# Inverse rms of an attention stage stored in 16-byte pieces, with the decay of v and the rms placed later in the step

## The chip, the cores and the metric

One core of one Trainium2 chip runs the whole program. The metric is the device time of one execution in microseconds (us). Engines are named as in the profile: PE (TensorE matmul), PEld (its weight load), DVE (VectorE), ACT (ScalarE), POOL (GpSimd), SP (SyncE, which here only issues DMAs). ACT issues some DMAs too; these go to a DMA queue of their own (q10 in the profile, SP's is q1).

## The reference, cut to what matters

Three layers follow each other: a retention attention over 4 x 8 heads of 576 positions, a gated feed-forward with an rms norm in front, and a mixture of 8 experts of which each token takes one.

```python
scores = scale * np.matmul(q, k.transpose(0, 1, 3, 2))
Dmat = np.where(rel >= 0, gamma[:, None, None] ** rel[None, :, :], 0.0)
attn = np.matmul(scores * Dmat, v)            # gamma by head, rel = row - column
x = attn.transpose(0, 2, 1, 3).reshape(2304, 512)
rms = np.sqrt(np.mean(x * x, axis=-1, keepdims=True) + 1e-06)
xn = x / rms * rms_g
g = xn @ w_gate
x2 = (g * (1.0 / (1.0 + np.exp(-g))) * (xn @ w_val)) @ w_out
# then: logits -> one expert per token -> relu(x2 @ w1[e]) @ w2[e], times the gate
```

## The kernel before, in words

**The attention stage** (lines 246 to 485) handles the 4 batches one after another, each in 5 chunks of 128, 128, 128, 128 and 64 positions: 20 steps, g = 0 to 19, and a last pass g = 20 that finishes step 19. The steps of 64 positions are g = 4, 9, 14 and 19. In pass g the program gives out:

- the loads of step g + 7 (`a_load`, on SP: qk L289 or L291, vk L296), because there are 8 buffers of each,
- the decay of step g + 2 (`a_decay` L302, POOL): v times gamma to the minus position, in place,
- the scores of step g (`a_scores`: PE L313, then DVE masks them into pt, L317),
- a DMA of inverse rms values that an earlier pass has left (`a_inv` L396, issued by ACT),
- the rms of step g - 3 (`a_norm1`), which does something only at the end of a group,
- the running state of step g (`a_state`: PE L332 adds into one PSUM tile st, two ACT copies L337 and L338 take it out),
- the output of step g - 1 (`a_pv`: PE L345 and L352, DVE scales it into x, L363; ACT squares it, L365; POOL adds the squares over channels, L373 and at a group's end L375),
- one piece of the background list bg0, then the store of x of step g - 3 (`a_store` L404, SP), then a piece of weight unpacking (`a_prep`, lines 130 to 148).

**Inverse rms.** The tokens of the four steps of 128 positions of a batch form a group, the four steps of 64 a fifth one; so groups end at g = 3, 8, 13, 18 and 19. At a group's end PE sums the squares over partitions (L386), ACT and DVE make the inverse rms (L388, L389): tile ri, 128 partitions by 4 values. It is written to the DRAM tensor rinv, 512 values in a row for each group, and read back by `load_inv` (L200), spread over all 128 partitions. The first block of the next stage, x0, is normalized within the attention stage: at g = LX0 ACT issues the load of its inverse rms, and from g = NX0 on one piece of bg0 is taken in each pass: first `norm_x` (DVE, L207), then four pieces of `split_x` (ACT L220 into xh, DVE L221 into xo).

**What sets the order.** Each engine runs its instructions in the order in which the program gives them out; SP and ACT do not go past a DMA issue that waits. Every DMA of SP and ACT also counts on one of eight completion counters, DMAHW0 to DMAHW7, taken in turn, and is issued only when the DMA that had the counter before has landed. x tiles of the attention stage have 5 buffers, so that the sixth x waits for the store of the first; st is one tile, so that L332 of a step waits for the ACT copies of the step before.

**The feed-forward stage** goes over 6 blocks of 512, 512, 512, 256, 256 and 256 tokens, each in 12 slices f of the inner dimension. The first block also unpacks the weights (DVE L137 to L143, ACT, POOL). The x of block j + 1 is normalized by `norm_x` during block j, from f = 5 on, one piece for each f. The experts follow. Neither their code nor the order in the feed-forward stage is touched, apart from `load_inv` and `norm_x`.

Of the kernel before, what the change touches and what calls it, by code (L numbers as in the profile page):

```python
# [13 lines left out]
ALU = mybir.AluOpType  # L14
# [6 lines left out]
KD = DM // 128  # L21
# [4 lines left out]
BLOCKS = [512, 512, 512, 256, 256, 256]  # L26
# [13 lines left out]
SD = 3  # L40
LS = 2
FX, FN = (3, 3), (5, 5)
LX0, NX0 = 9, 11
NUA = 4
PA, PS, LD, RB = 4, 3, 8, 4
NRW = 3
# [7 lines left out]
def kernel(  # L54
# [15 lines left out]
    PE, ACT, DVE, POOL, SP = nc.tensor, nc.scalar, nc.vector, nc.gpsimd, nc.sync  # L70
# [14 lines left out]
    def ps_g(name, dt=F32):  # L85
        return psum.tile([128, 512], dt, tag="gv", name=name, bufs=3)
# [5 lines left out]
    rinv = dram.tile([NT // 512 + 1, 512], F32, name="rinv")  # L92
# [103 lines left out]
    def load_inv(j, rl, q=SP):  # L196

        gr, o = divmod(STARTS[j], 512)
        w = min(512, NT - gr * 512)
        q.dma_start(out=rl[:, :w], in_=rinv[gr:gr + 1, :w].to_broadcast([128, w]))  # L200
        return rl[:, :w].rearrange("p (c t) -> p c t", t=128)[:, o // 128:(o + BLOCKS[j]) // 128]

    def norm_x(j, xl, rl):

        def scale(c):
            x, r = xl[:, c:c + 2], rl[:, c:c + 2]
            DVE.tensor_tensor(out=x, in0=x, in1=r.unsqueeze(2).to_broadcast([128, 2, KD, 128]), op=ALU.mult)  # L207

        return [lambda c=c: scale(c) for c in range(0, BLOCKS[j] // 128, 2)]

    def x_parts():
        return [
# [33 lines left out]
    with pool("att") as att:  # L246
# [18 lines left out]
        G = len(steps)  # L265
        qk_t, vk_t, pt_t, x_t, sums, bg0, inv = {}, {}, {}, {}, {}, [], []
# [13 lines left out]
        def by_pair(ps):  # L280
            return ps.rearrange("p (a t) -> p a t", a=NP)
# [17 lines left out]
        def a_decay(g):  # L299
            b, c, o, n = steps[g]  # L300
            v3 = vk_t[g][:n, 0, :].rearrange("p (h d) -> p h d", h=H)
            POOL.tensor_tensor(  # L302
                out=v3, in0=v3, in1=vd_c[:n, c, :].unsqueeze(2).to_broadcast([n, H, D]), op=ALU.mult
            )
# [35 lines left out]
        def a_pv(g):  # L340
            b, c, o, n = steps[g]
            qk, vk, pts = qk_t.pop(g), vk_t.pop(g), pt_t.pop(g)
            pv = by_pair(ps_g("pv"))
            for p in range(NP if c else 0):
                PE.matmul(  # L345
                    pv[:, p, :n], sbd[g % 3][:, p, :], qk[:, 0, p, :n],
                    start=(p == 0), stop=False, skip_group_check=True,
                )
            for p in range(NP):
                for a in range(2):  # L350
                    h = 2 * p + a
                    PE.matmul(  # L352
                        pv[64 * a:64 * a + 64, p, :n], vk[:n, 0, h * 64:h * 64 + 64], pts[a][:n, p, :n],
                        start=(c == 0), stop=True, skip_group_check=True,
                    )
            hc, ho = home(g)
            if hc < 2 * NS0:
                x = (x0 if hc < NS0 else x1)[:, hc % NS0]
            else:
                if not ho:  # L360
                    x_t[hc] = att.tile([128, NP, 128], F32, tag="x", name="x", bufs=XB)
                x = x_t[hc][:, :, ho:ho + n]
            DVE.tensor_tensor(out=x, in0=pv[:, :, :n], in1=rc[:, c, :, :n], op=ALU.mult)  # L363
            sq = att.tile([128, NP, 128], F32, tag="sq", name="sq", bufs=4)
            ACT.activation(out=sq[:, :, :n], in_=x, func=ACTF.Square)  # L365
            gr, o = place[g]
            if not o:
                if n == 128:
                    sums[gr[0]] = att.tile([128, 2, 512], F32, tag="sqs", name="sqs", bufs=2)
                else:  # L370
                    sums[gr[0]] = att.tile([128, 2, 256], F32, name="sqh")
            s = sums[gr[0]]
            POOL.tensor_tensor(out=s[:, :, o:o + n], in0=sq[:, 0:2, :n], in1=sq[:, 2:4, :n], op=ALU.add)  # L373
            if g == gr[-1]:
                POOL.tensor_tensor(out=s[:, 0, :], in0=s[:, 0, :], in1=s[:, 1, :], op=ALU.add)  # L375

        def a_norm1(g):

            gr, o = place[g]
            if g != gr[-1]:  # L380
                return
            n, sq = o + steps[g][3], sums.pop(gr[0])[:, 0, :]
            m = n // 128
            ss = ps_g("ss")
            for i in range(m):
                PE.matmul(ss[:, i:i + 1], sq[:, i * 128:i * 128 + 128], ones, start=True, stop=True)  # L386
            ri = att.tile([128, NS0], F32, tag="ri", name="ri", bufs=2)
            ACT.activation(out=ri[:, :m], in_=ss[:, :m], func=ACTF.Sqrt, scale=1.0 / DM, bias=eps[:, 0:1])  # L388
            DVE.reciprocal(out=ri[:, :m], in_=ri[:, :m])  # L389
            i = home(gr[0])[0] // NS0  # L390
            inv.append((rinv[i:i + 1, :n].rearrange("o (c t) -> t (o c)", c=m), ri[:, :m]))

        def a_inv():

# [23 lines left out]
        for k, stages in enumerate(ua):  # L418
            g = PA + PS * k
# [26 lines left out]
        for g in range(G + 1):  # L446
            if g + QB - 1 < G:
                a_load(g + QB - 1)
            if g + 2 < G:
                a_decay(g + 2)  # L450
            if g + 1 < len(CHUNKS):
                o, n = CHUNKS[g + 1]
                for p in range(NP):
                    i = g * NP + p
                    ACT.activation(
                        out=rc[:, g + 1, p, :n], in_=rc[:, 0, p, :n], func=ACTF.Copy, scale=adv[:, i:i + 1]
                    )
            if g < G:
                a_scores(g)
            a_inv()  # L460
            if g >= 3:
                a_norm1(g - 3)
            if g == LX0:
                bg0 += norm_x(0, x0, load_inv(0, rl0, ACT)) + split_x(x0, xsp, 512)
            if g < G:
                a_state(g)
            if g >= 1:
                a_pv(g - 1)
            if g >= NX0 and bg0:
                bg0.pop(0)()  # L470
            if g >= SD:
                a_store(g - SD)
            a_prep(g)
            if g == 3:
                SP.dma_start(out=kept, in_=keep)
            if g == 9:
                SP.dma_start(out=temp, in_=brief)
# [2 lines left out]
        assert not prep_a  # L480
        g0 = gv_mm(0, 0, xsp, BLOCKS[0])
        v0 = gv_mm(0, 1, xsp, BLOCKS[0])
        a_norm1(G - 2)
        a_norm1(G - 1)
        a_inv()

    wrest.append(ctx.enter_context(pool("wrest")))
# [278 lines left out]
    with pool("bp") as bp:  # L766
# [66 lines left out]
        for j, n in enumerate(BLOCKS):  # L833
            rate = -(-len(bg) // (NF if j < NB - 1 else LF))
            for f in range(NF):
# [8 lines left out]
                if f == FX[min(j, 1)] and j + 1 < NB:  # L844
                    x_in[:] = [load_x(j + 1) if j else x1]
                    rl = row_tile(F32, "rl") if j else wr[:, E - 1, :]
# [31 lines left out]
            if j + 1 < NB:  # L878
                bg, p1 = [], None
                for i in range(n // 128):  # L880
                    c = STARTS[j] // 128 + i
# [218 lines left out]
    with tc.For_i(0, n_left, 1) as i:  # L1100
# [19 lines left out]
            out=idx, in0=row[:, 520:521], scalar1=-1.0, scalar2=float(NT), op0=ALU.mult, op1=ALU.add  # L1120
# [7 lines left out]
        for f in range(NFF):  # L1128
# [13 lines left out]
            out=out[:, :], out_offset=bass.IndirectOffsetOnAxis(ap=idx[:, 0:1], axis=0),  # L1142
# [72 lines left out]
```

## Time and profile before

| | us |
|---|---|
| median of 3 runs (830.98 to 833.14) | 832.89 |
| the profiled execution's own time | 830.29 |
| its span | 828.5 |
| PE busy in the span | 799.7 (97%) |
| DVE, ACT, POOL busy | 478.0, 284.7, 152.0 |
| start of the first feed-forward matmul | 97.40 |

The attention stage is the first 97.40 us of the span. A busy PE is not PE at its peak: in this stage the matmuls are small and the granted clock (PEclk) changes. The waits of the stage are read from the timeline of PE and from the chain of work that ended last; what a DMA issue waits for, from the waits of SP.

### The profile page before, as it was taken

Reading aid. Unit: us, or ns where it says so; the run is one execution under the profiler, and the core shown is the slowest. Engines: PE = TensorE matmul, PEld = TensorE weight load, DVE = VectorE, ACT = ScalarE, POOL = GpSimd, SP = SyncE. Lnnn points to the kernel's source line nnn. Section 1 sums busy time; section 2 is a strip of 40 time slices with the busy share of each in tenths; the row PEclk is TensorE's granted clock in tenths of the full one; section 3 lists DMA queues with packets and bytes.
Section 4 is the critical chain, followed back from the end, with each engine's and each line's share of the span. In section 5 each row is a group of like instructions: output and inputs, shape, how many; then the busy total and the mean of one; then the engine's idle time right before and its main releaser. Section 6 shows DMA issues by size and latency. Waiting matters only on the chain.

```text
span 828.5 us, 13140 instructions
## 1 busy us (share of the span) xinstructions
PE 799.7 (97%) x4994; PEld 684.1 (83%) x4994; DVE 478.0 (58%) x1121; ACT 284.7 (34%) x538; POOL 152.0 (18%) x169
## 2 busy tenths in 40 slices
PE   8976999899999999999999999999999999999995
PEld 6865878677888888888899999999888898889894
DVE  3653568886455535454387653747474555566650
ACT  5432355555211131111311212134453444455540
POOL 4653436564000000000001000001000010011000
PEclk9987899999999999999999999999999999999998
DMA  9985576444910000000100100051735173767300
GB/s 342 314 281 185 130 206 225 151 153 168 387 42 14 14 27 25 14 15 13 52 15 27 46 14 14 14 201 56 256 125 195 52 251 117 293 230 253 124 19 13
DMA packets 40801, 105.12 MB, mean 127 GB/s; under 512 B 10462, under 2 KB 10974, under 8 KB 40608
## 3 DMA queue, kind: packets, MB, share of 16 engines
q1 hardware_dynamic: 34752, 93.87, 33.9%
q0 software_dynamic: 3168, 9.59, 3.0%
q10 hardware_dynamic: 2816, 0.80, 0.5%
q8 instruction: 40, 0.66, 0.3%
q14 instruction: 25, 0.20, 0.1%
HBM read 83.38 MB, written 21.78 MB: 127 GB/s over the span
## 4 chain that ended last, share of the span: by engine, by line
PE 77%; DVE 7%; DMA 5%; issue 5%; ACT 2%; POOL 1%; SPq 1%; ACTq 0%; another core or an unknown queue 0%; DVEq 0%; POOLq 0%
PE gv L229 10%; PE gv L231 10%; PE gv L230 10%; PE acc L229 10%; PE acc L230 10%; PE acc L231 10%; PE h L229 5%; PE h L230 4%; PE h L231 4%; DVE u L140 3%; DVE rawbt L137 2%; DMA rinv<-ri 2%; DMA vk<-in_vkn_dram 1%; PE tp L754 1%; DMA out_dram<-orow,idx 1%
## 5 line engine op out<-in xcount | busy, mean ns | idle before, releaser
L229 PE MATMUL gv<-xh,w 128*128 128x512 f32 (+1 forms) x576 | 196.5, 341 | 3.8 <-ACT scratch L777 3.5
L230 PE MATMUL gv<-xo,w 128*128 128x512 f32 (+1 forms) x576 | 194.3, 337 | 0.0
L231 PE MATMUL gv<-xh,w 128*128 128x512 f32 (+1 forms) x576 | 194.3, 337 | 0.0
L229 PEld LDWEIGHTS gv<-xh,w 128*128 128x128 f32 x576 | 109.3, 190 | 18.4 <-ACT scratch L777 5.3
L230 PEld LDWEIGHTS gv<-xo,w 128*128 128x128 f32 x576 | 109.5, 190 | 12.5
L231 PEld LDWEIGHTS gv<-xh,w 128*128 128x128 f32 x576 | 109.4, 190 | 11.9
L778 DVE TENSOR_TENSOR scratch<-gv,scratch 128x512 f32<-128x512 f32 (+1 forms) x72 | 40.0, 556 | 123.5 <-PE gv L231 119.7
L779 ACT CAST hh<-scratch 128x512 fp32r<-128x512 f32 (+1 forms) x72 | 37.0, 514 | 163.8 <-DVE scratch L778 163.8
L707 DVE TENSOR_TENSOR w<-raw,w 128x1024 fp32r<-128x1024 f32 x64 | 78.1, 1226 | 26.1 <-ACT w L706 25.1
L799 DVE CUSTOM_DVE_ANT_0 sink<-row,wr 128x512 bf16<-128x512 f32 x128 | 88.1, 689 | 2.6
L229 PE MATMUL h<-xt,w 128*128 128x256 f32 (+3 forms) x288 | 88.8, 308 | 0.0
L231 PE MATMUL h<-xt,w 128*128 128x256 f32 (+3 forms) x288 | 87.3, 303 | 0.0
L230 PE MATMUL h<-xt,w 128*128 128x256 f32 (+3 forms) x288 | 87.2, 303 | 0.0
L229 PE MATMUL acc<-wo,hh 128*128 128x512 f32 x216 | 86.0, 398 | 1.2 <-ACT hh L779 1.2
L231 PE MATMUL acc<-wo,hl 128*128 128x512 f32 x216 | 85.5, 396 | 0.0
L230 PE MATMUL acc<-wo,hh 128*128 128x512 f32 x216 | 85.4, 395 | 0.0
L777 ACT ACTIVATE scratch<-gv 128x512 f32<-128x512 f32 (+1 forms) x72 | 35.3, 490 | 136.0 <-PE gv L231 128.3
L549 POOL DMA_INDIRECT xs<-row,sloti x16 | 18.9, 1184 | 320.0 <-DVE lg L799 191.8
L706 ACT CAST w<-raw 128x1024 fp32r<-128x1024 f32 x64 | 65.9, 1041 | 1.4 <-DMA raw<-in_w_dram 1.4
L780 DVE TENSOR_TENSOR hl<-scratch,hh 128x512 fp32r<-128x512 f32 (+1 forms) x72 | 40.2, 559 | 42.0 <-ACT hh L779 42.0
L229 PE MATMUL acc<-w,rh 128*128 128x512 f32 (+1 forms) x160 | 63.6, 397 | 0.0
L230 PE MATMUL acc<-w,rh 128*128 128x512 f32 (+1 forms) x160 | 63.2, 395 | 0.0
(215 smaller groups left out, 1228.2 us busy)
## 6 DMA issues: line engine op xcount, KB each, us to landing
raw<-in_w_dram SPq DMA_DIRECT2D x64, 512.0 KB, 6.5
rawb<-in_wgv_dram SPq DMA_DIRECT2D x19, 512.0 KB, 5.6
xs<-zero SPq DMA_DIRECT2D x8, 1056.0 KB, 10.1
qk<-in_qkt_dram SPq DMA_DIRECT2D x16, 512.0 KB, 8.9
vk<-in_vkn_dram SPq DMA_DIRECT2D x16, 512.0 KB, 4.7
rowc<-xs SPq DMA_DIRECT2D x19, 264.0 KB, 5.8
rawb<-in_wout_dram SPq DMA_DIRECT2D x9, 512.0 KB
raw<-in_wgv_dram SPq DMA_DIRECT2D x4, 512.0 KB, 12.5
```

Source lines behind the costliest of these rows:

```text
L140: DVE.scalar_tensor_tensor(out=w, in0=hw, scalar=-0x40000000, in1=u, op0=ALU.bitwise_and, op1=ALU.bitwise_or)
L229: PE.matmul(ps, lh, rh, start=start, stop=False)
L230: PE.matmul(ps, lh, rl, start=False, stop=False)
L231: PE.matmul(ps, ll, rh, start=False, stop=stop)
L549: POOL.indirect_dma_start(out=xs[:, :], out_offset=bass.IndirectOffsetOnAxis(ap=sloti[:, 0:1], axis=0), in_=row[:, :], in_offset=None, bou ...
L706: ACT.copy(out=w[:, 0, :], in_=raw)
L707: DVE.tensor_tensor(out=w[:, 1, :], in0=raw, in1=w[:, 0, :].bitcast(F32), op=ALU.subtract)
L777: ACT.activation(out=h, in_=gps[:, :n], func=ACTF.Silu)
L778: DVE.tensor_tensor(out=h, in0=vps[:, :n], in1=h, op=ALU.mult)
L779: ACT.copy(out=hh[:, :n], in_=h)
L780: DVE.tensor_tensor(out=hl[:, :n], in0=h, in1=hh[:, :n].bitcast(F32), op=ALU.subtract)
L799: DVE.tensor_tensor_reduce(out=junk, in0=row[:, 0:DM].rearrange("p (a b) -> p a b", a=2), in1=wr[:, e, :].rearrange("p (a b) -> p a b", a= ...
```

## The change: what it does

- `a_inv`, `load_inv`: in a row of rinv the values stand token by chunk (t c) and no longer chunk by token (c t). A partition of ri so writes its four values as one piece of 16 bytes (8 in the last group), where it wrote four pieces of 4 bytes. The loaded row is viewed as chunk by token, with 16 bytes from one token to the next.
- `norm_x`: one DVE instruction for each chunk of 128 tokens, no longer for two.
- `a_decay` of step g + 2 is given out after `a_pv`, so that on POOL it stands behind the sums of step g - 1.
- the rms of a group is taken in the pass g + 4, no longer g + 3; the load of the first block's inverse rms moves from pass 9 to pass 10, the first background piece from pass 11 to 12.

```diff
-LX0, NX0 = 9, 11
+LX0, NX0 = 10, 12
@@ load_inv
-        return rl[:, :w].rearrange("p (c t) -> p c t", t=128)[:, o // 128:(o + BLOCKS[j]) // 128]
+        return rl[:, :w].rearrange("p (t c) -> p c t", t=128)[:, o // 128:(o + BLOCKS[j]) // 128]
@@ norm_x
         def scale(c):
-            x, r = xl[:, c:c + 2], rl[:, c:c + 2]
-            DVE.tensor_tensor(out=x, in0=x, in1=r.unsqueeze(2).to_broadcast([128, 2, KD, 128]), op=ALU.mult)
+            r = rl[:, c].unsqueeze(1).to_broadcast([128, KD, 128])
+            DVE.tensor_tensor(out=xl[:, c], in0=xl[:, c], in1=r, op=ALU.mult)
-        return [lambda c=c: scale(c) for c in range(0, BLOCKS[j] // 128, 2)]
+        return [lambda c=c: scale(c) for c in range(BLOCKS[j] // 128)]
@@ a_norm1
-            inv.append((rinv[i:i + 1, :n].rearrange("o (c t) -> t (o c)", c=m), ri[:, :m]))
+            inv.append((rinv[i:i + 1, :n].rearrange("o (t c) -> (o t) c", c=m), ri[:, :m]))
@@ the loop over the passes
-            if g + 2 < G:
-                a_decay(g + 2)
...
-            if g >= 3:
-                a_norm1(g - 3)
+            if g >= 4:
+                a_norm1(g - 4)
...
             if g >= 1:
                 a_pv(g - 1)
+            if g + 2 < G:
+                a_decay(g + 2)
...
-        a_norm1(G - 2)
-        a_norm1(G - 1)
+        for g in range(G - 3, G):
+            a_norm1(g)
```

On ACT, the first write of rinv (L396) and the load of the first block's inverse rms (L200) stood, before, with the work of passes 7 to 10 around them, as follows; sq is a square of x (L365), L337 and L338 are the copies of the state, raw and w8 belong to the unpacking.

```order
L365 ACTIVATE sq<-xl 128x512 [waits DVE_49,Pool_49]
L396 DMA rinv<-ri 128x4x1 [waits DMAHW6_49]
L337 COPY sbd2<-st 64x4x64 [waits PE_49]
L338 COPY sbd2<-st 64x4x64
L365 ACTIVATE sq<-xl 128x512 [waits DVE_49,Pool_49]
L136 ACTIVATE raw<-raw 128x512 [waits DMAHW0_49]
L337 COPY sbd0<-st 64x4x64 [waits PE_49,Activation_49]
L338 COPY sbd0<-st 64x4x64 [waits Activation_49]
L365 ACTIVATE sq<-xl 128x512 [waits DVE_49,Pool_49]
L147 CAST w8<-rawt 128x512
L200 DMA rl0<-rinv 128x512 [waits DMAHW6_49]
L365 ACTIVATE sq<-xl 128x512 [waits DVE_49,Pool_49]
```

In the changed kernel the same place on ACT reads:

```order
L136 ACTIVATE raw<-raw 128x512 [waits DMAHW0_49]
L396 DMA rinv<-ri 128x4 [waits DMAHW1_49]
L337 COPY sbd0<-st 64x4x64 [waits PE_49,Activation_49]
L338 COPY sbd0<-st 64x4x64 [waits Activation_49]
L365 ACTIVATE sq<-xl 128x512 [waits DVE_49,Pool_49]
L147 CAST w8<-rawt 128x512
L365 ACTIVATE sq<-xl 128x512 [waits DVE_49,Pool_49]
L200 DMA rl0<-rinv 128x512 [waits DMAHW7_49,DMAHW1_49]
L337 COPY sbd2<-st 64x4x64 [waits PE_49,Activation_49]
L338 COPY sbd2<-st 64x4x64 [waits Activation_49]
```

The write moved behind the square of step 6 and an unpacking piece (it goes out in pass 8, not 7). The load moved behind the square of step 8, the last of the second group; behind it stand now the state copies of step 10. Both times the load waits for the counter of the write, 6 before and 1 now.

On SP, the loads of step 14 to 17 stood before as follows (raw and temp are weights and constants). The second row, vk of step 14, waits for counter 6, which the load of rl0 has; the last row, qk of step 17, waits for counter 5, which the second write of rinv has.

```order
L291 DMA qk<-in_qkt_dram 128x8x64 [waits DMAHW6_49,DMAHW4_49,PE_49]
L296 DMA vk<-in_vkn_dram 64x512 [waits DMAHW6_49,PE_49,Pool_49]
L289 DMA qk<-in_qkt_dram 128x1024 [waits DMAHW7_49,PE_49]
L296 DMA vk<-in_vkn_dram 128x1024 [waits DMAHW0_49,PE_49,Pool_49]
L131 DMA raw<-in_wout_dram 128x1024 [waits DMAHW1_49,DVE_49]
L289 DMA qk<-in_qkt_dram 128x1024 [waits DMAHW2_49,PE_49]
L296 DMA vk<-in_vkn_dram 128x1024 [waits DMAHW3_49,PE_49,Pool_49]
L477 DMA temp<-in_brief_dram 128x180 [waits DMAHW4_49]
L289 DMA qk<-in_qkt_dram 128x1024 [waits DMAHW5_49,PE_49]
```

In the changed kernel these rows are, from the raw weights ahead of step 13 to vk of step 15, and from qk of step 18 to the first store of x:

```order
L131 DMA raw<-in_wgv_dram 128x1024 [waits DMAHW1_49]
L289 DMA qk<-in_qkt_dram 128x1024 [waits DMAHW2_49]
L296 DMA vk<-in_vkn_dram 128x1024 [waits DMAHW3_49,PE_49,Pool_49]
L291 DMA qk<-in_qkt_dram 128x8x64 [waits DMAHW4_49,PE_49]
L296 DMA vk<-in_vkn_dram 64x512 [waits DMAHW5_49,PE_49,Pool_49]
L289 DMA qk<-in_qkt_dram 128x1024 [waits DMAHW6_49,PE_49]
L296 DMA vk<-in_vkn_dram 128x1024 [waits DMAHW7_49,PE_49,Pool_49]
...
L289 DMA qk<-in_qkt_dram 128x1024 [waits DMAHW7_49]
L296 DMA vk<-in_vkn_dram 128x1024 [waits DMAHW0_49,PE_49,Pool_49]
L291 DMA qk<-in_qkt_dram 128x8x64 [waits DMAHW1_49,PE_49]
L296 DMA vk<-in_vkn_dram 64x512 [waits DMAHW2_49,PE_49,Pool_49]
L404 DMA xnd<-x 128x512 [waits DMAHW3_49,DVE_49]
```

SP's own rows have not moved; the writes of rinv now fall on other counters. The first write has counter 1, for which the raw weights wait; the load of rl0 has counter 7, for which vk of step 15 waits; the second write has counter 0, for which vk of step 18 waits, three rows ahead of the first store.

## Rows read from the trace of the kernel before

**Rows 1.** Timeline of PE: start us, us, engine, line, operation, tiles, count, [idle before <-releaser]
```profile
43.48 1.16 PE L313 MATMUL sc<-qk 64*128 64x128 f32 x16
49.47 1.87 PE L386 MATMUL ss<-ones,sqs 128*128 128x1 f32 x8 [4.83 <-POOL sqs L375]
...
83.60 1.12 PE L332 MATMUL st<-vk 128*64 128x64 f32 x16 [5.96 <-POOL vk L302]
...
97.40 0.50 PE L229 MATMUL gv<-xh,w 128*128 128x512 f32 x1
```

**Rows 2.** Windows: stretch, busy us by engine (instructions), PEclk, DMA share, GB/s
```profile
20.00:30.00 10.00, 9.59 (x152) 8.52 (x149) 6.70 (x14) 5.66 (x11) 7.89 (x9) 1.00 1.05 381
30.00:40.00 10.00, 10.00 (x152) 8.80 (x150) 6.72 (x12) 4.46 (x9) 6.08 (x8) 1.00 1.13 271
40.00:50.00 10.00, 5.17 (x79) 4.53 (x75) 4.37 (x8) 2.33 (x5) 4.63 (x5) 0.87 0.92 263
120.00:240.00 120.00, 115.32 (x495) 91.49 (x494) 87.89 (x158) 52.28 (x91) 48.89 (x32) 1.00 0.58 204
240.00:560.00 320.00, 320.00 (x1829) 277.16 (x1828) 176.78 (x541) 69.34 (x143) 24.02 (x50) 1.00 0.10 34
```

**Rows 3.** Chain that ended last, in order of time: start us, us, what
```profile
27.29 1.05 PE ss L386 x8
...
30.69 15.18 DMA rinv<-ri
...
45.89 0.34 ACTq L200
...
46.63 0.64 ACT sq L365
...
47.34 0.73 POOL sqs L373
...
48.14 1.28 POOL sqs L375
...
58.00 1.09 PE sc L313 x16
59.09 0.61 PE st L332 x16
59.71 1.09 PE pv L345 x8
60.80 1.05 PE pv L352 x16
...
66.76 1.04 POOL vk L302
...
74.77 6.16 DMA xnd<-x
...
81.02 0.44 DVE x L363
```

**Rows 4.** Waits of SP's queue in the first 130 us: in total, times, longest
```profile
SPq L289 <- DMA rinv<-ri: 13.1, 1, 13.1
...
SPq L296 <- DMA rl<-rinv: 10.5, 1, 10.5
```

**Rows 5.** Instructions on the tensor rinv
```profile
DMA to landing us min/median/max: 9.4/9.4/9.4
```

**Rows 6.** Timeline of DVE
```profile
59.79 1.28 DVE L317 TENSOR_TENSOR pt<-sc,soon 128x512 f32<-128x512 f32 x2
61.87 0.69 DVE L363 TENSOR_TENSOR x<-pv,soon 128x512 f32<-128x512 f32 x1 [0.80 <-PE pv L352]
63.93 0.75 DVE L221 SCALAR_TENSOR_TENSOR xo<-x,kept,xh 128x512 fp32r<-128x512 f32 x1 [1.37 <-ACT xh L220]
```

**Rows 7.** Instructions by line, L207
```profile
L207 DVE TENSOR_TENSOR xl<-xl,wr x2: 1491/1495/1499, 162.4 to 172.0; 128x1024 f32<-128x1024 f32 x2
```

## Prediction

> **What bounds the kernel now.** I looked at the span first, then at the stages, then at the one stage in which PE stands. From 240 to 560 us, the later feed-forward blocks, PE has no gap [rows 2], and nothing of the change touches the experts. What is left is the attention stage, the first 97.40 us [rows 1], and the first feed-forward block, where DVE is busy for 87.89 of 120 us and PE for 115.32 [rows 2].
>
> In the attention stage I read the timeline of PE for its stops. There are two large ones: 4.83 us ahead of the sum ss at 49.47, and 5.96 us ahead of the state matmuls at 83.60 [rows 1]. After each stop PE is also slow for a while: ss takes 1.87 where it took 1.05 before the first stop, the state matmuls take 1.12 at 83.60 and 0.61 at 59.09 [rows 1, 3], and the granted clock from 40 to 50 us is 0.87, below the upper one of its two levels [rows 2].
>
> How much the stops cost altogether comes from counting work. A full pass of 128 positions takes PE 1.09 + 0.61 + 1.09 + 1.05 = 3.84 us [rows 3]. A pass with the scores of a 64-position step takes about 2.7 (0.6 for the scores, 2.14 for the output of the step before); the pass after it about 3.3, since that output is short; a pass behind the first step of a batch 2.75, since the output then needs no L345. From the scores of step 11 at 43.48 [rows 1] there remain passes 11 to 20: 2.75, 3.84, 3.84, 2.74, 3.34, 2.75, 3.84, 3.84, 2.74 and 1.64, with two sums ss of 1.05: 33.4 us. They took 97.40 - 43.48 = 53.9. So 20.5 us are stops and slow clock, nearly all of what a change to this stage can give.
>
> Then the chain of waits, for who ends the stops. The first: the write of inverse rms, issued by ACT at 30.69, lands after 15.18 us. The load L200 waits for it at the head of ACT's queue until 45.89; only then come the square of step 8 (46.63), its sum on POOL (47.34), the group's sum (48.14), and with it PE's ss [rows 3]. The second runs over SP: one load (L289) waits 13.1 us for a write of rinv [rows 4]. By the order it is qk of step 17, which shares a counter with the second write. Behind it in SP's queue stands the first store of x, which goes out only at 74.77 and lands 6.16 us later; DVE's x at 81.02 waits for its buffer [rows 3], ACT's square and the state copies wait for DVE, PE's st for the copies. A third wait of SP, 10.5 us for the load of rl0 [rows 4], holds vk of step 14 back. All three come from how long a write of 2 KB takes: 15.2 us among other loads, 9.4 with little beside it [rows 3, 5]. While the first is under way the DMA engines are as busy as before but move 271 GB/s, after 381 [rows 2].
>
> **The change part by part.**
>
> *The write.* It has 128 pieces for 512. If the pieces alone set the time, the 9.4 us become 2.4; if they do not matter, 15.2 stays [rows 3, 5]. The nearest row is the store of x, also 128 pieces from 128 partitions to DRAM, which lands after 6.16 us behind several loads [rows 3]. I take 6.2, and keep both ends for the range. The Trainium skill ("DMA: Bandwidth & Descriptors", Specifications) speaks against it: below 512 bytes an engine reads, modifies and writes, and 16 bytes are as far below as 4. By that each piece costs what it did, and a quarter of the pieces a quarter of the 9.4 us; only if the cost is not by the piece does the first rival below follow from it. The trace has no 16-byte write that could tell.
>
> *The rms a pass later.* The write goes out one pass and an unpacking piece later, at about 30.69 + 4.6 = 35.3, and lands at 41.5. L200 now stands behind the square of step 8: pass 10 takes 3.34 and begins at 43.48 - 3.34 = 40.1, x takes 0.69 [rows 6] and the square 0.64 [rows 3], so ACT reaches L200 at 41.5 as well, and does not stand. What is queued behind it are the state copies of step 10, for which PE's st of step 11 waits at 44.6; this is 3 us of slack. The first stop and its slow clock go. One new thing on SP: the raw weights ahead of step 13 wait for the first write, until 41.5; steps 11 and 12 are ahead of them in the queue and step 13 is needed at 51, so this costs nothing.
>
> *Decay behind the sums.* Of 18 moved decays only those behind a group's sum are tight: step 11's comes at 41.5 + 0.73 + 1.28 + 1.04 [rows 3] = 44.6, and with an unpacking piece of POOL ahead, taken as 0.73, at 45.3. PE wants st at 44.6: +0.8 with the counter's signal. Elsewhere the decay has a pass more, or the data come early: 0.
>
> *The second write.* It goes out behind the square of step 11: passes 11 and 12 end at 43.48 + 2.75 + 4.89 + 0.8 = 51.9, and with 0.69 + 0.64 this is 53.3. It lands at 59.5. For it waits vk of step 18, with two more loads and then the store of step 9 behind; store out at 61, landed at about 67. DVE wants that buffer (x of step 14) at the end of pass 15: 51.9 + 3.84 + 2.74 + 3.34 = 61.8. So DVE still stands for 5 us, but most is hidden: after it come a short square (about 0.4) and two state copies (about 0.8), so st of step 17 is free at 68.4, where PE arrives at 61.8 + 2.75 + 1.09 + 1.05 = 66.7: +1.7. This term follows the landing of the second write one to one.
>
> *The splits of x0 three passes later*, in 16 to 19 and no longer 13 to 16. In such a pass DVE needs x 0.69, 1.37 of waiting for ACT, xo 0.75 and pt 1.28 [rows 6] = 4.1. Four passes and an unpacking unit (three instructions, estimated at 0.69 each) make 18.5, PE's passes 16 to 19 14.2 with ss. DVE runs up to a pass ahead, which covers about 1.2: +3.1.
>
> *Half pieces of norm_x.* In block 0 two instructions of 1.495 us [rows 7] become four of about 0.75: DVE is the late one there [rows 2], so the extra starts count, +0.2. Later blocks: 0, since DVE has 176.78 of 320 us to do there and PE no gap [rows 2]. How a 16-byte step in the loaded row reads on DVE no row shows; the lower end is no cost, the upper one a piece twice as long, 4 x 0.75 = 3.0; I take 0, since the rows of 512 values differ little by operand, 0.69 from PSUM and 0.75 with a cast [rows 6].
>
> The sum on the profiled execution: 830.29 - 20.5 + 0.8 + 1.7 + 3.1 + 0.2, and 0.5 for a slow clock after the waits that stay, is 816.1. The median of the runs shown is 2.6 above that execution, so I predict 818.7.
>
> **The rivals.**
>
> 1. *The write stays as long* (slower). Its price is then per write and not per piece. It goes out at 35.3, lands at 50.5, and L200 holds the state copies of step 10 and so st of step 11 until 51.3, where it stood before too (ss at 49.47, then st); but ss of the group still has to be done in pass 12 (+1.05), and the second write, a pass later, lands about 4 us later than before; three loads instead of six ahead of the store make up half of that (+2). 832.9 + 3 = 836. It decides from a landing of about 12 us on. For it: no row tells the time of the pieces from the wait for their landing. Against: 15.2 us is far above the 6.16 of a store of 128 times as many bytes [rows 3].
>
> 2. *The decay loop takes over.* x, square, sum, decay is now one chain of 0.69 + 0.64 + 0.73 + 1.04 = 3.1 us from a pass's output to the state of the pass after next, 4.4 at a group's end, and it inherits each delay of DVE and ACT. PE gives it between 3.8 and 4.9. With DVE late in the passes with a split or an unpacking unit, 8 passes lose about 1 us each: 818.7 + 8 = 826.7. For it: DVE's 4.1 us a pass. Against: before, POOL waited for DMA more than for ACT.
>
> 3. *The stepped reading costs.* Four pieces in block 0 twice as long: +3.0, and x0's four in the attention stage partly: 822. The Trainium skill ("SBUF — State Buffer", the paragraph on cachelines in Door 1) says that SBUF has lines of 16 bytes and that an access that moves to a new line each time pays. By that this rival holds, since every value would lie on a new line. No row here has such an operand.
>
> 4. *The loads stay held.* Writes are short, but SP still meets a counter at a bad place, at three new rows; the stops move and do not go: 832.
>
> **How the numbers follow.** Forecast 0.60, 812 to 823. Rival 1 0.11, rival 2 0.17, rival 3 0.08, rival 4 0.04. If all 20.5 us came back it would be 830.29 - 20.5 + 2.6 = 812.4, and half of the spread of the runs below that, 811, is the lower end; the upper one, 830, takes in rival 2 with 1.4 us lost in each of the 8 passes, and leaves out rivals 1 and 4, 0.15. The least change that can be told from none is 0.3%, 2.5 us, so: faster 0.87 (forecast, rivals 2 and 3, and a little of rival 4), same 0.05 (rivals 4 and 1 near their break-even), slower 0.08 (rival 1).
>
> **What would show it right or wrong.** Writes of rinv that land within 8 us; L200 issued near 42 with no wait; no stop of PE over 1 us ahead of ss of the second group; the store of step 9 out near 61; the first feed-forward matmul at about 82.5; the distance from there to the end of the span unchanged within 1 us. Wrong would be: a landing over 10 us, st waiting for POOL in most passes, DVE's pieces of norm_x over 1 us, or block 0 longer by what the attention stage gains.

## The result and the profile after

After takes 820.28 us (median of 4 runs, 819.86 to 820.97); before, run beside it, 832.31 (830.98 to 833.14). The ratio is 0.9858, 95% interval 0.9841 to 0.9875. The forecast was 818.7.

| | before | after |
|---|---|---|
| profiled execution, us | 830.29 | 819.86 |
| its span | 828.5 | 818.1 |
| first feed-forward matmul | 97.40 | 84.70 |
| from there to the end of the span | 731.1 | 733.4 |
| DVE busy | 478.0 | 486.7 |

The edit of the write shows in the page's count of DMA packets, 39137 where 40801 stood: 1664 fewer, which is 384 for each of the four full writes and 128 for the last. The attention stage is 12.7 us shorter, the rest 2.3 longer. The timeline of PE after (columns as in [rows 1]):

```profile
43.61 1.16 PE L313 MATMUL sc<-qk 64*128 64x128 f32 x16
45.44 0.69 PE L332 MATMUL st<-vk 128*64 128x64 f32 x16 [0.67 <-POOL vk L302]
...
65.83 0.78 PE L332 MATMUL st<-vk 128*64 128x64 f32 x16 [2.80 <-POOL vk L302]
66.39 1.93 PE L352 MATMUL pv<-pt,vk 128*64 128x128 f32 x16
68.25 1.83 PE L313 MATMUL sc<-qk 64*128 64x128 f32 x16
...
80.12 0.43 PE L352 MATMUL pv<-pt,vk 128*64 128x128 f32 x2 [0.59 <-DVE pt L317]
80.72 1.09 PE L352 MATMUL pv<-pt,vk 128*64 128x128 f32 x14 [0.17 <-DVE pt L317]
...
83.81 0.96 PE L352 MATMUL pv<-pt,vk 64*64 64x64 f32 x16 [0.97 <-issue]
84.70 0.50 PE L229 MATMUL gv<-xh,w 128*128 128x512 f32 x1
```

The stops of 4.83 and 5.96 us [rows 1] are gone. One of 2.80 is new, ahead of the state matmuls of step 16, for the decay of v; after it PE is slow for two instructions. The windows (columns as in [rows 2]) show it as a granted clock of 0.83, and the first write no longer as a hole in the transfers: 370 GB/s, where 271 stood.

```profile
30.00:40.00 10.00, 10.00 (x144) 8.96 (x144) 6.33 (x12) 5.68 (x11) 5.41 (x7) 1.00 1.04 370
40.00:50.00 10.00, 9.33 (x153) 8.27 (x150) 7.66 (x12) 3.99 (x9) 7.38 (x8) 1.00 0.71 237
...
60.00:70.00 10.00, 7.20 (x90) 6.37 (x88) 6.61 (x12) 3.02 (x7) 5.89 (x6) 0.83 0.91 309
```

The landing of a write, from the instructions on rinv [rows 5: 9.4]:

```profile
DMA to landing us min/median/max: 7.0/7.0/7.0
```

What SP waits for (columns as in [rows 4]): the load held by the second write waits 4.5 us, where qk of step 17 waited 13.1.

```profile
SPq L131 <- DMA rinv<-ri: 10.8, 2, 5.4
...
SPq L296 <- DMA rinv<-ri: 4.5, 1, 4.5
```

Where the 2.3 us after the attention stage lie is read from ACT: the first instruction on each slice's gate product, L777. Slices 6, 10 and 11 of the first block, before:

```profile
160.84 0.59 ACT L777 ACTIVATE scratch<-gv 128x512 f32<-128x512 f32 x1
...
196.51 0.59 ACT L777 ACTIVATE scratch<-gv 128x512 f32<-128x512 f32 x1
...
199.74 0.60 ACT L777 ACTIVATE scratch<-gv 128x512 f32<-128x512 f32 x1 [1.25 <-PE gv L231]
```

and after:

```profile
148.01 0.60 ACT L777 ACTIVATE scratch<-gv 128x512 f32<-128x512 f32 x1
...
185.87 0.59 ACT L777 ACTIVATE scratch<-gv 128x512 f32<-128x512 f32 x1
...
188.86 0.60 ACT L777 ACTIVATE scratch<-gv 128x512 f32<-128x512 f32 x1 [1.02 <-PE gv L231]
```

The five slices from slice 6 to slice 11 take 38.90 us before and 40.85 after, +1.95. The first four of them, in which all pieces of norm_x stand, take 35.67 and 37.86, +2.19; the fifth takes 3.23 and 2.99. From the first gate product to slice 6 it is 53.5 us in both. The pieces of norm_x [rows 7], by line after (min/median/max ns, first and last start):

```profile
L207 DVE TENSOR_TENSOR xl<-xl,rl x10: 684/1080/1094, 243.4 to 477.2; 128x512 f32<-128x512 f32 x10
L207 DVE TENSOR_TENSOR x<-x,rl x4: 1065/1100/1279, 52.5 to 67.8; 128x512 f32<-128x512 f32 x4
L207 DVE TENSOR_TENSOR xl<-xl,wr x4: 1336/1342/1352, 149.5 to 180.1; 128x512 f32<-128x512 f32 x4
```

A piece of half the size costs 1.342 us in block 0, nine tenths of the whole one of before (1.495). The pieces of 684 ns are those of the last block, whose group has two values per token, so a step of 8 bytes and not 16.

### The profile page after: what moved, and what is told of

It is laid out like the page before. It is cut to its first block, busy times and chain, and to the rows that moved or that the text cites. A ratio compares the mean times of both kernels' runs of the same rounds, so it can differ in the third digit from the quotient of the medians.

```text
span 818.1 us, 13148 instructions
## 1 busy us (share of the span) xinstructions
PE 794.1 (97%) x4994; PEld 678.5 (83%) x4994; DVE 486.7 (59%) x1130; ACT 284.6 (35%) x538; POOL 154.0 (19%) x169
## 2 busy tenths in 40 slices
DMA packets 39137, 105.12 MB, mean 128 GB/s; under 512 B 8798, under 2 KB 9310, under 8 KB 38944
## 4 chain that ended last, share of the span: by engine, by line
PE 79%; DVE 9%; issue 5%; DMA 4%; ACT 2%; POOL 1%; SPq 0%; another core or an unknown queue 0%; DVEq 0%; ACTq 0%; POOLq 0%
PE gv L229 10%; PE gv L231 10%; PE gv L230 10%; PE acc L229 10%; PE acc L231 10%; PE acc L230 10%; PE h L229 5%; PE h L230 5%; PE h L231 5%; DVE u L140 3%; DVE rawbt L137 2%; PE pv L352 1%; PE tp L754 1%; PE pv L345 1%; DMA raw<-in_wout_dram 1%
## 5 line engine op out<-in xcount | busy, mean ns | idle before, releaser
L229 PE MATMUL gv<-xh,w 128*128 128x512 f32 (+1 forms) x576 | 196.4, 341 | 4.1 <-ACT scratch L777 3.7
L229 PEld LDWEIGHTS gv<-xh,w 128*128 128x128 f32 x576 | 109.4, 190 | 18.5 <-ACT scratch L777 5.5
L229 PE MATMUL h<-xt,w 128*128 128x256 f32 (+3 forms) x288 | 88.8, 308 | 0.0
L229 PE MATMUL acc<-wo,hh 128*128 128x512 f32 x216 | 86.2, 399 | 1.9 <-ACT hh L779 1.9
L777 ACT ACTIVATE scratch<-gv 128x512 f32<-128x512 f32 (+1 forms) x72 | 35.4, 491 | 134.4 <-PE gv L231 129.3
L934 POOL DMA_INDIRECT out_dram<-orow,idx x22 | 23.5, 1067 | 218.8 <-ACT ex L731 78.2
L229 PE MATMUL acc<-w,rh 128*128 128x512 f32 (+1 forms) x160 | 63.6, 397 | 0.0
```

The source lines that it names most:

```text
L229: PE.matmul(ps, lh, rh, start=start, stop=False)
L777: ACT.activation(out=h, in_=gps[:, :n], func=ACTF.Silu)
L934: POOL.indirect_dma_start(out=out[:, :], out_offset=bass.IndirectOffsetOnAxis(ap=idx[:m, i:i + 1], axis=0), in_=orow[:m, :], in_offset=Non ...
```

## The experiments

The times are medians; the two probes, e5 and e9, ran once and stand at the end. The other columns are from one trace of each run. "Five slices" is the stretch from slice 6 to slice 11 above, "first four" the part of it up to slice 10; "x(14)" the start of DVE's x of step 14, which waits for the store of step 9.

| run | us | ratio, 95% interval | x(14) | first gv | five slices | first four |
|---|---|---|---|---|---|---|
| before | 832.31 | | 81.02 | 97.40 | 38.90 | 35.67 |
| after | 820.28 | 0.9858 (0.9841 to 0.9875) | 67.42 | 84.70 | 40.85 | 37.86 |
| e1 the layout alone | 819.53 | 0.9863 (0.9831 to 0.9895) | 68.45 | 85.13 | 40.40 | 37.17 |
| e2 all but the layout | 831.92 | 1.0005 (0.9986 to 1.0024) | 80.82 | 97.78 | 40.24 | 36.30 |
| e3 decay at the head | 819.95 | 0.9870 (0.9837 to 0.9904) | 66.91 | 84.21 | 41.40 | 37.85 |
| e4 8-byte pieces | 821.53 | 0.9872 (0.9835 to 0.9909) | 70.02 | 86.92 | 40.21 | 36.30 |
| e6 before, 8-byte | 819.36 | 0.9876 (0.9848 to 0.9904) | 67.57 | 83.95 | 40.44 | 35.63 |
| e7 after, 8-byte, two chunks | 821.63 | 0.9906 (0.9878 to 0.9935) | 69.81 | 87.38 | 38.92 | 35.66 |
| e8 rms early | 822.37 | 0.9906 (0.9875 to 0.9936) | 67.76 | 86.83 | 40.80 | 37.84 |
| e10 after, six x | 820.12 | 0.9854 (0.9831 to 0.9876) | 64.02 | 86.93 | 41.43 | 37.88 |
| e11 8-byte, decay at the head, six x | 817.39 | 0.9827 (0.9811 to 0.9843) | 66.22 | 83.57 | 38.88 | 35.65 |
| e12 before, 8-byte, six x | 816.06 | 0.9807 (0.9790 to 0.9823) | 64.18 | 82.38 | 40.45 | 35.65 |

The first four slices have four levels. They take 35.6 to 35.7 us with whole pieces, packed or with an 8-byte step (before, e6, e7, e11, e12), 36.30 with half pieces (e2, e4), 37.17 with whole pieces and a 16-byte step (e1), and 37.8 to 37.9 with both (after, e3, e8, e10). So the cut costs 0.6 us, the 16-byte step 1.5, both 2.2. The fifth slice holds no piece; what it adds depends on whether the clock fell just before it. It takes 3.2 us at full clock in before, e1, e7 and e11 and 3.0 in after and e8, but 3.55 in e3 and e10, 3.9 in e2 and e4, and 4.8 in e6 and e12 (granted 0.60 from 180 to 183 us in e6). The window of e2 from its slice 9 to its slice 10 (columns as in [rows 2]; 1.00 in after at the same place):

```profile
192.10:198.98 6.88, 6.24 (x20) 4.97 (x21) 5.29 (x9) 2.83 (x6) 3.50 (x2) 0.75 0.00 0
```

**e1 and e2: which part gains.** e1 is before with the two rearranges of the layout and nothing else; e2 is after with them undone. Cut to the two expressions:

```diff
-rinv[i:i + 1, :n].rearrange("o (c t) -> t (o c)", c=m)
+rinv[i:i + 1, :n].rearrange("o (t c) -> (o t) c", c=m)
-rl[:, :w].rearrange("p (c t) -> p c t", t=128)
+rl[:, :w].rearrange("p (t c) -> p c t", t=128)
```

> The kernel before with one edit: rinv in token-by-chunk order, so that a write has 128 pieces of 16 bytes; decay, rms and background pieces stand where they stood before. If the pieces make the gain: the first write lands about 7 us after its issue at 30.7, ACT does not stand at L200, PE has no stop of over 1 us ahead of ss of the second group, the first feed-forward matmul comes at 83 to 86, and the whole takes 817 to 823 us. If the moved decay and rms make it: 830 to 835. If a 16-byte step in the operand is slow on DVE: the two L207 of the first feed-forward block take 2.4 to 2.7 us each instead of 1.5.

> The changed kernel with one part undone: rinv is written in 512 pieces of 4 bytes again; decay behind the sums, rms a pass later and half pieces of norm_x stay. If the pieces make the gain: landings of 14 to 16 us, ACT stands at L200 until about 50, st of step 11 waits 5 to 7 us, and the whole takes 832 to 837 us (836 by the first rival of the prediction). If the order makes the gain: 819 to 823. The half pieces of L207 read packed values here: 0.68 to 0.78 us each, where the 16-byte step took 1.08 to 1.34.

The layout alone gives the whole gain: in e1 ACT reaches L200 at 40.56 and does not stand there. The order alone gives none, and it does not lose 3 us either, as rival 1 had it. The waits of e2 were shorter than expected: ACT is held at L200 until 46.06 and not 50, and st of step 11 waits 2.71 and not 5 to 7. In e2 the writes land after 11.5 and 13.4 us (14 to 16 were expected), vk of step 18 stands behind the second one, and PE stops for 6.49 us ahead of a group's sum where before it stopped for 5.96 elsewhere:

```profile
SPq L296 <- DMA rinv<-ri: 12.0, 1, 12.0
```

Pieces of norm_x in e1 (two chunks, 16-byte step; 2.25 us, half as much again as packed, a little under the 2.4 to 2.7 expected), then in e2 (one chunk, packed):

```profile
L207 DVE TENSOR_TENSOR xl<-xl,wr x2: 2246/2252/2258, 149.1 to 159.5; 128x1024 f32<-128x1024 f32 x2
```

```profile
L207 DVE TENSOR_TENSOR xl<-xl,rl x10: 683/684/685, 257.4 to 491.3; 128x512 f32<-128x512 f32 x10
...
L207 DVE TENSOR_TENSOR xl<-xl,wr x4: 954/957/961, 164.2 to 193.6; 128x512 f32<-128x512 f32 x4
```

**e3: the decay back at the head of the pass**, the rest as after.

> The changed kernel with the decay of step g + 2 given out at the head of the pass again. If the decay behind the sums holds st (waits of 0.42, 0.67 and 2.80 us for POOL in the changed kernel, with slow clock behind the last): these waits go, the first feed-forward matmul comes 3 to 5 us earlier, the whole takes 815 to 818 us. If instead the moved decay is what keeps the sums ahead of ss: a wait of 0.5 to 2 us ahead of ss at the group ends, and 820 to 823.

A miss in size. PE no longer waits for the decay (0.89 us are left ahead of st of step 16, where ACT's state copies end at 63.80), but DVE is late next: stops of 0.95 (pt), 0.94 and 0.76 (x), 0.49, 0.60 us. The first gv comes 0.5 sooner and the time is the same.

**e4: pieces of 8 bytes.** After, with the row of rinv as "o (h t c)", c = 2: two chunks side by side, 256 pieces.

> The changed kernel with rinv written in pairs of chunks: 256 pieces of 8 bytes, and 8 bytes from one token to the next in the loaded row. If the landing goes with the number of pieces: between that of 128 pieces (7.0) and of 512 (15.2), 9 to 11 us, and ACT stands at L200 for 2 to 4 us. If it goes with nothing below 16 bytes: about 7. The pieces of L207 take 0.68 to 0.80 us if two values in 16 bytes are enough for DVE (the 8-byte step of the last block took 0.68), and the first feed-forward block becomes 2 us shorter; 1.1 to 1.3 if any step costs. Whole: 818 to 824, since the two effects are opposed.

The writes land after 8.0 and 8.2 us, between the two expectations, and the pieces of norm_x are as short as packed ones (684 and 954 ns): an 8-byte step costs nothing, a 16-byte step 0.4 us a piece. The five slices fall only to 40.21, which is e2's 40.24. Against before 0.6 of the remaining 1.3 us is the cut, by the first four slices; the other 0.7 is the fifth slice behind a fallen clock. The four times of e4 spread from 818.5 to 824.0, and its trace is of the longest.

**e6 and e7: two chunks a piece again**, with the 8-byte layout, in the order of before (e6) and of after (e7).

> The kernel before, with one change: the inverse rms is written in 256 pieces of 8 bytes (two chunks side by side) and read with a step of 8 bytes, norm_x still in two pieces of two chunks. Theory: the gain is the shorter landing alone and the loss in block 0 is the split of norm_x into four pieces (1.3 us) and the 16-byte step (0.6 us), so nothing is lost here: norm_x pieces 1.49 to 1.50 us, the five steps from feature tile 7 to 11 of block 0 sum to 38.9 us as before (after: 40.85), landing of the first write about 8 us and no stand at L200, first gv at 85 to 86, time 817.5 to 819.5. Rival: an 8-byte step costs too where two chunks are read at once: pieces about 1.9 us (16-byte step: 2.25), five steps 39.7, time 819.5 to 821. Rival: 256 pieces land too late for the reader: a stand of ACT at L200 of over 1 us, time over 822.

> The kernel after, with 256 pieces of 8 bytes and norm_x in two pieces of two chunks: against the run with 8-byte pieces (821.53 us, five steps 40.21) only the number of norm_x pieces differs. Theory: the four pieces cost 1.3 us in block 0, so the five steps are 38.9 us and the time is 819.5 to 821. Rival: the number of pieces is nothing and the 1.3 us comes with the new order of decay and rms: steps stay 40.2, time 821.5.

The pieces are 1.492 and 1.500 us, as before. e7's five slices are 38.92, as expected, but not for the reason expected: the cut is 0.6 of the 1.3 us, and the clock did not fall. Its time missed the range by 0.6: st waited 1.73 and 3.08 us for the decay, and the first gv came at 87.38. So against after, what the slices gained the attention stage lost. e6, in before's order, is no slower than after; its five slices missed 38.9 by the slow clock named above, its first gv came sooner than expected (83.95 for 85 to 86), and its first write landed after 7.7 us with no stand at L200.

**e8: rms at g - 3, L200 at step 9**, the rest as after.

```diff
-            if g >= 4:
-                a_norm1(g - 4)
+            if g >= 3:
+                a_norm1(g - 3)
...
-LX0, NX0 = 10, 12
+LX0, NX0 = 9, 11
```

> The kernel after with the rms of a group taken at step g-3 again and norm_x a step earlier (L200 at step 9): the third part of the change undone alone. Theory: with a write that lands in 7 us the place of the rms decides nothing: first write out at 32.3 us, no stand at L200, first gv within 0.7 us of 84.7, time 819.3 to 821.3. Rival: a step later is worth something (work of the step before no longer waits behind Sqrt and reciprocal): without it a stand at L200 or on SP of over 1 us, time 822 or more.

The rival's time came, by a mechanism that neither had named: L200 does not stand, and though a load waits 6.0 us for a write (5.4 at most in after), x(14) comes only 0.3 us later. Rows of DVE, POOL and PE in e8:

```profile
67.76 0.42 DVE L363 TENSOR_TENSOR x<-pv,soon 128x256 f32<-128x256 f32 x1 [5.67 <-DMA xnd<-x]
```

```profile
69.19 1.04 POOL L302 TENSOR_TENSOR vk<-vk,soon 128x512 f32<-128x512 f32 x1
```

```profile
70.34 1.12 PE L332 MATMUL st<-vk 128*64 128x64 f32 x16 [3.79 <-POOL vk L302]
```

PE is not stopped at step 16 here, so it reaches step 17 sooner and waits there for what the store of step 9 holds: x(14), its square, and the state copies and the decay behind it. That is the chain for which the prediction put +1.7. In after it is hidden behind the stop at step 16.

**e10 to e12: a sixth buffer for x** (XB = 6), so that x(14) waits for no store. e10 is after, e12 is e6, e11 is e7 with the decay at the head of the pass.

> The kernel after with six buffers for x in place of five, so that x of step 14 waits for no store. In nine traces so far the first feed-forward matmul starts 16.4 to 19.1 us after that x. Theory 'store': the landing of the first store (67.3 us) sets the end of the attention stage, so without the wait (3.39 us of DVE) x of step 14 comes at 64 to 65 and the first gv 1.5 to 2.5 us sooner, 82.2 to 83.2; st of step 16 still waits about 2.8 us for the decay; time 818 to 819. Rival 'decay': the stop ahead of st of step 16 sets the end, the store's wait lies behind it: first gv 84.4 to 85, time 820.3.

> The kernel before with 8-byte pieces and six buffers for x (the run with 8-byte pieces and five: 819.36 us, first gv at 83.95, x of step 14 held 1.53 us by the store). Theory 'store': x of step 14 comes 1.5 us sooner, first gv at 82 to 83.2, time 817 to 818.5. Rival: PE's stops there (ss waiting for POOL 1.28, pv for DVE 0.52) come from DVE's own work, and the first gv stays within 0.5 us of 83.95: time 819 to 820.

> 8-byte pieces, norm_x in two pieces of two chunks, the decay at the head of the pass again, rms a pass later, and six buffers for x: each part as the runs so far speak for it. Theory: neither the decay nor the store stops PE; what is left is DVE in the passes with a split (1 to 1.5 us before pv); first gv at 81 to 82.5, five steps of block 0 38.9 us, time 815.5 to 818. Rival: the slow clock or DVE take the place of each stop that goes, and the first gv stays at 84 to 85: time 818 to 820.

In the trace of e10, neither. x(14) comes at 64.02, but its normalizing piece (16-byte step, 1.40 us) now runs beside the decay of step 16 on POOL. Rows of POOL, of PE and of the windows in e10:

```profile
64.79 1.87 POOL L302 TENSOR_TENSOR vk<-vk,soon 128x512 f32<-128x512 f32 x1
```

```profile
66.72 1.12 PE L332 MATMUL st<-vk 128*64 128x64 f32 x16 [3.64 <-POOL vk L302]
```

```profile
70.00:80.00 10.00, 10.00 (x85) 8.97 (x82) 5.58 (x9) 3.65 (x8) 2.37 (x3) 0.53 0.08 31
```

The decay takes 1.87 us for 1.04, the stop is 3.64 for 2.80, and after it the clock stays at its lower level through nearly the whole window of 70 to 80. The first gv comes at 86.93, 2.2 later than in after. The median says little here: the four times are 818.7, 818.8, 821.5 and 821.6, and the trace is of the last, with a mean granted clock of 0.986 where the two shorter have 0.992. The shorter two lie where the theory had them; whether the clock fell in them too, no trace shows.

In e12, with the decay at the head, the sixth buffer is worth 3.3 us (816.06 against e6's 819.36), somewhat more than the range expected; the first gv is in its range. Between the two traces it is 2.4 us: 1.6 up to the first gv, and 1.0 in the first slices of block 0, where an L140 on DVE beside POOL takes 1.86 us in e6 and none over 0.70 in e12. One stop over 1 us is left from step 10 on:

```profile
64.24 1.86 PE L387 MATMUL ss<-ones,sqs 128*128 128x1 f32 x8 [2.08 <-POOL sqs L376]
...
82.38 0.50 PE L230 MATMUL gv<-xh,w 128*128 128x512 f32 x1
```

e12 beats both kernels: 4.2 us below after, the intervals apart. e11's time fell in its range, its first gv did not (83.57; st waits 1.73 and 1.50). e11 and e12 are not told apart.

**e5 and e9: what a small write costs.** In after, with the transfers idle in block 1, writes from one tile to DRAM, each followed by a read-back that waits for it; its issue less the write's issue is the landing. Cut to the two DMAs, as e5 has them; e9 adds the pitch:

```diff
+ SP.dma_start(out=to, in_=kept[:, 0:c * e].rearrange("p (c e) -> p c e", c=c))
+ SP.dma_start(out=back[0:1, :], in_=pw[i][:, 0:16])
```

> The kernel after, and in block 1 at feature tile 7 (the transfers idle there) six writes from one tile in on-chip memory to device memory, each followed by a read-back that has to wait for it: 512 pieces of 4 bytes, 128 of 16, 512 of 16, 128 of 4, 256 of 8, 128 of 512. Theory 'count': the landing goes by the number of pieces, so 512x4 and 512x16 are alike (9 to 10 us, as the uncontended write of before took 9.4) and 128x4, 128x16 and 128x512 are alike (2.5 to 4 us), 256x8 between (4 to 6). Theory 'size': what costs is a piece under 512 bytes, so 128x512 is clearly shorter than 128x16, and 512x16 shorter than 512x4 by the same rule per byte. Time of the whole: 820 to 850 us, it says nothing.

> The kernel after, and in block 1 at feature tile 7 six writes to device memory, each followed by a read-back that waits for it, as in the first probe (there 512x4 bytes side by side took 8.5 us, 128x4 7.3, 256x8 4.1, 512x16 2.7, 128x16 2.3, 128x512 1.7: not by count, and not by 512 bytes). Now: 128 pieces of 4 bytes side by side; the same 128 with a pitch of 16, 64 and 512 bytes; 128 pieces of 16 bytes with a pitch of 64; 512 pieces of 4 bytes with a pitch of 64. Theory 'neighbours': pieces that lie close together in memory wait for one another, so the first is again 7 to 7.6 us, the pitch of 16 falls to 2.2 to 2.8 (as 128x16 side by side) and 64 and 512 to 1.7 to 2.2, the 512 pieces with a pitch of 64 to 2 to 3. Theory 'small piece': a 4-byte piece costs what it costs wherever it lies, so all four of 128x4 are 7 to 7.6 us and the 512 with a pitch of 64 8 to 9. Time of the whole 818 to 823 us, it says nothing.

e5 on SP's queue (start us, us of the issue): 128 x 16 bytes, then (after the dots) 128 x 4 bytes, both side by side in DRAM.

```profile
226.89 0.36 SPq L855 DMA_DIRECT2D pw<-kept  x1
229.14 0.24 SPq L856 DMA_DIRECT2D back<-pw  x1
...
232.43 0.34 SPq L855 DMA_DIRECT2D pw<-kept  x1
239.75 0.23 SPq L856 DMA_DIRECT2D back<-pw  x1
```

e9: 128 x 4 bytes side by side, then 128 x 4 with a pitch of 64 bytes, then 512 x 4 with a pitch of 64.

```profile
218.98 1.28 SPq L855 DMA_DIRECT2D pw<-kept  x1
227.13 0.30 SPq L856 DMA_DIRECT2D back<-pw  x1
...
230.06 0.33 SPq L855 DMA_DIRECT2D pw<-kept  x1
231.51 0.24 SPq L856 DMA_DIRECT2D back<-pw  x1
...
235.29 0.38 SPq L855 DMA_DIRECT2D pw<-kept  x1
237.22 0.24 SPq L856 DMA_DIRECT2D back<-pw  x1
```

| side by side | us | apart | us |
|---|---|---|---|
| 512 x 4 bytes | 8.5 | 512 x 4, pitch 64 | 1.93 |
| 128 x 4 | 7.3 and 8.2 | 128 x 4, pitch 64 | 1.45 |
| 256 x 8 | 4.1 | 128 x 4, pitch 512 | 1.46 |
| 128 x 16, 512 x 16 | 2.3, 2.7 | 128 x 4, pitch 16 | 2.31 |
| 128 x 512 | 1.7 | 128 x 16, pitch 64 | 1.47 |

e5 refutes 'count'. Of 'size' the direction holds, but not the place: going from 16 to 512 bytes a piece saves 0.6 us, from 4 to 16 it saves 5. e9 decides for neighbours. A quarter of the pieces of 4 bytes takes nearly as long (of its 8.2 us in e9 the issue itself is 1.28), four times the pieces of 16 hardly longer, and pieces of 4 bytes that lie 64 bytes apart cost nothing extra. What is slow is 16 pieces within 64 bytes; with 8 there it is 4.1 us, with 4 it is 2.3. No pitch between 16 and 64 was tried, so whether 64 bytes or 32 is the unit stays open. In the kernel, among the loads, the first write with 16, 8 and 4 pieces in 64 bytes lands after 11.5 to 15.2 (e2, before), 7.7 to 8.0 (e6, e4) and 7.0 us (after): the same order, but most of the 7.0 is not the pieces. So, by the probes, after's write is faster because four pieces and not 16 share 64 bytes; that there are fewer of them hardly counts.

## Why the prediction was right, and where it was off

*The write* was taken as 6.2 us and measured 7.0 and 7.3. The prices by the piece (9.4 to 2.4) and the row taken gave nearly the right size for a wrong reason, and that is luck: 512 pieces of 16 bytes land in 2.7 us where 128 take 2.3, so the number hardly counts, and the rest of the 7.0 came in the kernel, among the loads. The Trainium skill ("DMA: Bandwidth & Descriptors", Specifications), held against it, says that writes under 512 bytes are read, modified and written; here 128 pieces of 4 bytes with a pitch of 64 land in 1.45 us and 128 of 512 bytes in 1.7, so smallness by itself has no price that shows.

*The times of the chain* held. Forecast and measured: first write out 35.3 and 34.66, landed 41.5 and 41.65, L200 at 41.65 without a wait; second write out 53.3 and 52.66, vk of step 18 out 59.5 and 60.00; first store out 61 and 61.55, landed 67 and 67.3. Both big stops went, as said.

*Decay of step 11*: 0.8, measured 0.67.

*"Elsewhere the decay has a pass more, or the data come early: 0"* is a step that failed. The decay of step 16 also stands behind a group's sum, and PE waited 2.80 us for it. The rows of POOL in after:

```profile
62.61 0.82 POOL L373 TENSOR_TENSOR sqs<-sq 128x256 f32<-128x256 f32 x1 [3.44 <-ACT sq L365]
63.51 1.26 POOL L375 TENSOR_TENSOR sqs<-sqs 128x512 f32<-128x512 f32 x1
64.73 1.04 POOL L302 TENSOR_TENSOR vk<-vk,soon 128x512 f32<-128x512 f32 x1
```

and of DVE, whose x at 61.13 starts that chain:

```profile
57.30 0.97 DVE L137 TENSOR_SCALAR rawt<-raw 128x512 int32<-128x512 int32 x1
58.30 1.42 DVE L140 SCALAR_TENSOR_TENSOR u<-raw,rawt 128x512 int32<-128x512 int32 x1
```

PE's output of step 13 ended at 58.3; its x came 2.8 us later, because an unpacking unit and a stepped normalizing piece (1.10) stood ahead, and its second instruction, begun 0.35 us after a decay on POOL, took 1.42 us where the same one takes 0.70 at 103.86. This is rival 2's mechanism, at one place instead of eight. e3 shows the other side: with the decay at the head PE waits for DVE, for less each time but more often.

*The store of step 9 into st of step 17* (+1.7) is real, as e8 shows (3.79), but in after lies behind the stop at step 16 and costs nothing of its own. Taking away either alone (e3, e10) moves the median by nothing that can be told. That the two stops hide each other is argued from this and not shown: after with both taken away and nothing else changed was not run.

*The splits of x0*: 3.1, measured 0.59 + 0.17 + 0.97 = 1.7. *Slow clock*: 0.5, measured 1.5 (pv 1.93 for 1.09, sc 1.83 for 1.16). Together, from the scores of step 11 at 43.61 to the first gv the stage takes 41.1 us for 33.4 of work: 7.7 us of stops and slow clock where the terms said 6.1. The measured terms make 6.7; where the last 1.0 lies is not worked out. That the sum came so near is luck in part: 1.7 for the store and 1.4 of the splits did not come, and 2.80 for the decay and 1.0 of slow clock came unforeseen. The first gv was due at 82.5 or, with the slow clock, 83.0, and came at 84.70.

*Half pieces of norm_x* (+0.2, and 0 for the step) measured +1.95, nearly all of the error behind the attention stage. Both its parts were wrong, the step most. A piece of 512 values is not half of 1.495 us but 0.957 packed (e2), four of them 3.83 for 2.99; and the step of 16 bytes, taken at 0, makes it 1.342. Measured by the first four slices: 0.63 for the cut (e2 less before), 1.50 for the step (e1 less before), 2.19 for both; the fifth slice gave 0.24 back. Rival 3 had the step right in kind, at half its price of 3.0. Its rule holds: the Trainium skill ("SBUF — State Buffer", the paragraph on cachelines) asks for at least two accesses to a line of 16 bytes. By that an 8-byte step is free and a 16-byte step is not; the rows agree: 0.684 and 1.08 us for the same piece. The same paragraph counts four fp32 values as a free stride, which these rows contradict at exactly four.

On the profiled execution the sum was 816.1 and the trace 819.86: 3.8 us off, about 1.7 in the attention stage and 2.1 behind it. The median was 1.6 off, since after's lies only 0.4 above its profiled execution and I had added before's 2.6: two errors that partly cancel. Of the signs that the prediction named, the distance from the first gv to the end of the span failed (+2.3, not within 1), and one of the signs of being wrong came: pieces of norm_x over 1 us.

*The rivals.* Rival 1 needed a landing of 12 us; it was 7.0. e2 shows what such landings would have given: 832, not 836. Rival 4 did not come: no load stands behind a write for over 5.4 us.

What stays open: whether e1, e3, e6 and after differ at all (819.4 to 820.3); why the clock after a stop is back within 5 us in after and only after some 12 in e10; and why in block 0 a stop of 2.02 us ahead of L229 at 192.74 is followed by the lower clock in e2, and one of 2.04 at the same place in after is not.

## What to carry to other kernels

Where a small write to DRAM is waited for, look at how its pieces lie in memory, not at their number or its bytes: regroup until few pieces share 64 bytes, and take the widest group that the reader can still read two values at a time. Before cutting an instruction in two, or giving an operand a step, find a row of that size and step; half of the whole, and nothing for the step, were both too little. Compare like stretches before splitting a difference: with the slice of the fallen clock left in, the cut looked like 1.3 us and the step like 0.6, where they are 0.6 and 1.5. And when several waits end near each other, price them together: the sixth buffer did not show in the median beside the late decay (e10), and with the decay at the head it was worth 3.3 us (e6 to e12).

## What the runs showed of the hardware

- Pieces of 4 bytes side by side in DRAM: 7.3 to 8.5 us to land, whether 128 or 512 of them; at a pitch of 64 bytes 1.5 to 1.9 (e5, e9, with the transfers idle).
- DVE reading an operand with a step of 8 bytes is as fast as packed (0.684 us for 128x512), with 16 bytes 1.08.
- DVE and POOL slow each other, mostly the one that begins second: in after, L140 begun 0.09 us ahead of POOL's L148 takes 0.70 and L148 1.75 (at 103.86), begun 0.01 behind it 1.85 and L148 1.31 (at 107.86). The Trainium skill ("SBUF — State Buffer", Terms) has the two share a pair of ports that one of them holds for a whole instruction; these rows nearly agree: an estimate by it, the later one's own time and the rest of the other's, is 1.92 and 2.00 for the 1.75 and 1.85. The second pair:

```profile
107.85 1.31 POOL L148 TENSOR_TENSOR w<-rawbt,w 128x512 fp32r<-128x512 f32 x1 [2.14 <-DVE rawbt L137]
107.86 1.85 DVE L140 SCALAR_TENSOR_TENSOR u<-rawb,rawbt 128x512 int32<-128x512 int32 x1
```

- A stop of 2.80 us was followed by two slow instructions of PE, one of 3.64 by a clock of 0.53 for the window from 70 to 80 us.
